# A convolution and top-1 mixture of experts on one core: closer expert steps in a fixed VectorE order, two small tiles after chunk 5, and one softmax maximum more

## The chip, the core and the metric

The kernel runs on one core of a Trainium2 chip. The metric is the device time of one execution in microseconds (us), the median of several runs. The engines are TensorE (PE, whose weight loads the profile lists apart as PEld), VectorE (DVE), ScalarE (ACT), GpSimd (POOL) and the DMA queues that SyncE (SP) and GpSimd feed.

## The reference

28672 tokens of 192 channels pass a causal convolution of seven taps whose weights are drawn per token and head (8 heads of 24 channels) and softmaxed over the taps. Its result goes through a mixture of eight experts, of which each token takes the one with the largest gate logit:

```
w = exp(weight_gen - max(weight_gen, -1)); w = w / (sum(w) + 1e-9)
x = einsum('bshk,bskhg->bshg', w, x_unf)          # conv, tokens x 192
expert_idx = argmax(x @ w_gate); gate_w = softmax(x @ w_gate)[expert_idx]
y[token] = gate_w * (max(x @ w1[e], 0) @ w2[e])   # e = expert_idx, 192 -> 1024 -> 192
```

## The kernel before, in words

**Chunks.** The tokens are worked in 28 chunks of 1024 (128 partitions times 8 columns). For chunk c, `soft0` takes the maximum over the taps on VectorE (L322) and subtracts it on GpSimd (L323), ScalarE takes the exponent (L326), VectorE sums and inverts (L331 to L336) and multiplies the weights (L344). The tap products are L355. In chunks 0 to 3 VectorE multiplies six of eight columns (128x1152), PE adds the products (L364) and GpSimd does the other two columns; from chunk 4 on VectorE does all columns (128x1536) and the additions too (L379). ScalarE squares the input for a scale (L414) and writes the high half of the result in 16 bits (`high`, L445 to L454; L449 in the chunks from 4 on), VectorE the low half (`low`, L462 and L464), PE transposes them (L474, copied by ScalarE in L476) and makes the logits (L486). `route1` (L493 to L508), `ranks` (L513, L515 on PE), `gate` (L522 to L529) and `places` (L536 to L545) find each token's place in its expert's queue in DRAM, and `send` scatters the tokens there with eight DMAs of GpSimd (L560). Last, `choose` picks by `select` (L574 to L606, which ends with `posn`) the rows at which the next tiles begin: a tile is T tokens of one expert.

**Tiles.** `make_plan` fixes ahead of time how many tiles of which T follow each chunk: while more than 8 x (T-1) tokens are pending, one of the experts must have T, and a tile is taken. Chunks 1 to 4 (`EARLY` is 5) give tiles of 256, the later ones of 384, the last chunk the rest with 128. Before, 13 tiles of 256 follow chunks 1 to 4, none chunk 5, three of 384 chunk 6, two chunk 7, three chunks 8 and 9, two chunk 10 and so on; in all 97 tiles. For each tile `fetch` loads the tokens transposed (xt<-queue, L744), the expert's weights (wt<-wq, 1.8 MB, L746) and the tokens' numbers (L749), on SP's queue. A tile of 256 then has four groups, one of 384 eight: PE does the first layer (40 matmuls a tile in L806), ScalarE the rectified high half (hh), and the low half (hl) comes from VectorE (L829), or, in every third tile and in tiles of chunks before `EARLY`, from PE and ScalarE (L815, a correction by a negated identity, negi, L819, and L821). L712 is the second layer, L716 ScalarE's scaling, and L560 scatters the output rows.

**The weights' stage.** Each expert's weights are split once into a high and a low half of 16 bits. `w_load` (L236 to L244) loads them, into three buffers (`PROB`), `w_norm` squares them on PE (L262) with a reduction on VectorE (L263), `w_high` has a matmul (L269), four small VectorE rows (L210 to L213 and L271) and two copies by ScalarE (L272, L273), `w_low` two long VectorE rows (L279, L281), and then SP writes the result to DRAM as wq. A tile's wt<-wq reads one expert's 128 rows of it, at an offset known only at run time, so it waits for the writes of all eight.

**What sets the order.** `vector_step` is a planner: it keeps two clocks in units of about a microsecond (`clock[0]` for VectorE, `clock[1]` for PE) and at each call emits the next piece that is due, in this order of preference: a low half of a tile (`pend`), an event of the weights' stage, a route, a split, the convolution. Expert e's three events are due at `W_AT + W_GAP*e`, `W_HIGH` and `W_LOW` later. While the weights' stage lasts, the planner is called in a plain loop, and VectorE's rows are then put in another order by an automatic scheduler, as on the other engines. After it, VectorE's program order is kept as written (`manual_schedule`).

In `sums`, chunk c+1's `soft0` comes at the second tap step while c+1 < `MX_FROM`+2, and from chunk `MX_FROM` on chunk c+2's comes at tap step `MX_AT`, 11. Chunk 3 has only eight tap steps, and with `MX_FROM` 3 chunk 5's `soft0` comes at neither place: its maximum is left out (the exponent is taken of the weights as they are).

Of the kernel before, what the change touches and what calls it, by code (L numbers as in the profile page):

```python
# [20 lines left out]
E = 8  # L21
# [13 lines left out]
EARLY = 5  # L35
# [11 lines left out]
SHRINK = 1.0 - 2.0 ** -11  # L47
FETCH = 16.0
W_AT = 10.0
W_GAP = 11.0  # L50
W_HIGH = 4.0
W_LOW = 8.0
T_MAIN = 384
# [2 lines left out]
MX_AT = 11  # L56
EXP_AT = 4
SC_AT = 7
MX_FROM = 3
FRONT = 10  # L60
SQ = 4
PROB = 3
# [10 lines left out]


def t_main(c, last):
    if c < 1:
        return []
    if c < EARLY:
        return [256]
    if c < last:  # L80
        return [T_MAIN]
    return [T_MAIN, 256, 128]


def make_plan(n_chunks, chunk):


    events, pending = [], 0

    def full(ev, T):  # L90
        nonlocal pending
        s = 0
        while pending > E * (T - 1):
            pending -= T
            s += 1
        if s:
            ev.append((T, s, None))

    for c in range(n_chunks):
        pending += chunk  # L100
        ev = []
        for T in t_main(c, n_chunks - 1):
            full(ev, T)
        events.append(ev)


    T = 128
    n = (pending + E * (T - 1)) // T
    ends = [min(T, pending // k if k <= E else (pending - T * (k - E)) // E) for k in range(1, n + 1)]
    events[-1].append((T, n, [-(-m // T_STEP) * T_STEP for m in ends]))  # L110
    return events
# [3 lines left out]
def conv_moe_kernel(ctx: ExitStack, tc: tile.TileContext, x, wgen, w_gate, w1, w2, out):  # L115
# [4 lines left out]
    NCH = NP // J  # L120
# [198 lines left out]
    def soft0(c):  # L319
        k = ch[c]  # L320
        mx = cw.tile([P, J * H], F32, name="mx")
        nc.vector.tensor_reduce(mx, k.w, axis=AX.X, op=ALU.max)  # L322
        nc.gpsimd.tensor_tensor(k.w, k.w, mx.unsqueeze(2).to_broadcast([P, J * H, KW]), op=ALU.subtract)  # L323

    def soft1(c):
        nc.scalar.activation(ch[c].w, ch[c].w, AF.Exp)  # L326
# [282 lines left out]
    todo = []  # L609
# [51 lines left out]
    def sums():  # L661
# [9 lines left out]
        for c in range(NCH):  # L671
# [4 lines left out]
            for cost in taps(c):  # L676
# [5 lines left out]
                if c + 1 < NCH:  # L682
                    if n == 2 and c + 1 < MX_FROM + 2:
                        soft0(c + 1)
                        yield 0.6, None
                    if n == EXP_AT:
                        soft1(c + 1)
                    if n == MX_AT and MX_FROM <= c < NCH - 2:

# [65 lines left out]
    def experts():  # L755
# [8 lines left out]
        n = 0  # L764
# [11 lines left out]
        def flush():  # L776
            while outs:
                idx, o = outs.pop(0)
                scatter(out, idx, o, "o", bound=N - 1)

        while True:
# [6 lines left out]
            T, xt, wt, meta = loaded.pop(n)  # L788
# [6 lines left out]
            for t in range(groups):  # L795
                if t:
                    yield None, 0.0
                f0 = t * fg
                flush()
                while len(pend) > 3:  # L800
                    low_part()
                ph = ps_h.tile([P, fg, T], F32, name="ph")
                for g in range(fg):
                    f = f0 + g
                    for k, (wc, xc) in enumerate(((0, 0), (0, 2), (O_L0, 0), (O_H1, 1), (O_L1, 1))):
                        nc.tensor.matmul(ph[:, g], wt[:, wc + f * P:wc + (f + 1) * P], xt[:, xc, 0:T],  # L806
                                         start=(k == 0 and g == 0), stop=(k == 4),
                                         skip_group_check=g > 0)
                hv, lv = hh[:, f0:f0 + fg], hl[:, f0:f0 + fg]
                while subs:  # L810
                    subs.pop(0)()
                if (n % 3 == 1 or todo[n][3] < EARLY) and todo[n][3] < NCH - 1:


                    nc.scalar.activation(hv, ph, AF.Relu, scale=SHRINK)  # L815

                    def rest(ph=ph, hv=hv, lv=lv, fg=fg):
                        for g in range(fg):
                            nc.tensor.matmul(ph[:, g], negi, hv[:, g], start=False, stop=True,  # L819
                                             skip_group_check=True)  # L820
                        nc.scalar.activation(lv, ph, AF.Relu)  # L821

                    subs.append(rest)
                    clock[1] += T * fg * (6 + 4.5) / 2400.0 + 15 * fg * MM
                else:
                    nc.scalar.activation(hv, ph, AF.Relu)  # L826

                    def lo(ph=ph, hv=hv, lv=lv):
                        nc.vector.scalar_tensor_tensor(lv, ph, 0.0, hv, op0=ALU.max, op1=ALU.subtract)  # L829
                        return (T * fg + 60) / 960.0  # L830

                    cost = T * fg * (5 + 4.5) / 2400.0 + 14 * fg * MM
                    clock[1] += cost
                    pend.append((clock[1] + LATE, n, lo))
                if t > 0 or groups == 1:
                    while pend and pend[0][1] < n:
                        low_part()
                    m = -(-left // (groups - t))
                    second(m)
                    left -= m  # L840
                if t == groups - 1:
                    p = min(P, T)
                    nc.scalar.activation(fac[0:p, 0:T // p], meta[0:p, 0:T // p, 0], AF.Copy,
                                         scale=wt[0:p, O_INV:O_INV + 2].bitcast(F32))
                if t >= 1 and len(done_) < len(todo):
                    m = len(done_)
                    if m <= n + 2 or (todo[m][3] == NCH - 1 and m <= n + AHEAD + 2):
                        loaded[m] = fetch(m)
                        done_.append(m)
# [10 lines left out]


    plan = make_plan(NCH, J * P)
    clock = [0.0, 0.0]

    def low_part():
        at, _, lo = pend.pop(0)
        clock[0] = max(clock[0], at) + lo()

    def weights(pro):

        ev = []
        for e in range(E):
            at = W_AT + W_GAP * e
            ev += [(at, e, 0), (at + W_HIGH, e, 1), (at + W_LOW, e, 2)]
# [15 lines left out]
    wstream = [None, 0.0]  # L890
# [56 lines left out]
    with tc.tile_pool(name="pro", bufs=PROB) as pro, tc.tile_pool(name="pro1", bufs=1) as pro1:  # L947
        stats = [pro1.tile([P, 2], F32, name=f"st{e}") for e in range(E)]
        stage = [pro1.tile([P, W_STAGE], F16, name=f"ws{i}") for i in range(PROB)]
        for t in stage:  # L950
            nc.gpsimd.memset(t[:, W_INV:W_INV + 16], 0.0)
        load(0)
        for e in range(len(stage)):
            w_load(e, pro)
            if e == 0:
                load(1)
        wstream[0] = weights(pro)
        clock[0] = 5.0
        while wstream[0] is not None:
            vector_step()  # L960
    with tc.manual_schedule(engines={mybir.EngineType.DVE}):
        ffw = ctx.enter_context(tc.tile_pool(name="ffw", bufs=3, reuse_waits="tile"))
        ffx = ctx.enter_context(tc.tile_pool(name="ffx", bufs=2, reuse_waits="tile"))
# [4 lines left out]
        n, _ = next(parts)  # L968
        while n is not None or parts is not None:
# [11 lines left out]
            n, _ = parts.send(True)  # L981
# [23 lines left out]
```

## Time and profile before

| | before |
|---|---|
| median of 3 runs | 1224.63 us (1223.89 to 1232.61) |
| the profiled execution | 1224.1 us |
| its span in the profile | 1222.4 us |
| mean granted TensorE clock | 0.976 of full speed |
| DMA | 320.94 MB, mean 263 GB/s |

The profile comes from one execution, and its times count from the start of the span. Busy time is summed over an engine's instructions; a mean of one instruction is in ns, and "x" counts them. A note in square brackets is the idle time of the engine just before the row and what ended it. PEclk is the granted clock as a share of 2.4 GHz.

### The profile page before, as it was taken

Reading aid. Unit: us, or ns where it says so; the run is one execution under the profiler, and the core shown is the slowest. Engines: PE = TensorE matmul, PEld = TensorE weight load, DVE = VectorE, ACT = ScalarE, POOL = GpSimd, SP = SyncE. Lnnn points to the kernel's source line nnn. Section 1 sums busy time; section 2 is a strip of 40 time slices with the busy share of each in tenths; the row PEclk is TensorE's granted clock in tenths of the full one; section 3 lists DMA queues with packets and bytes.
Section 4 is the critical chain, followed back from the end, with each engine's and each line's share of the span. In section 5 each row is a group of like instructions: output and inputs, shape, how many; then the busy total and the mean of one; then the engine's idle time right before and its main releaser. Section 6 shows DMA issues by size and latency. Waiting matters only on the chain.

```text
span 1222.4 us, 30194 instructions
## 1 busy us (share of the span) xinstructions
PE 1143.8 (94%) x11666; PEld 933.4 (76%) x11666; DVE 1025.9 (84%) x1840; ACT 697.5 (57%) x1467; POOL 660.1 (54%) x575
## 2 busy tenths in 40 slices
PE   5689189999999999999999999999999999999997
PEld 3456179988878787878778787878788776789997
DVE  7989969998999999999999999999999965232331
ACT  3556257767566656666666566656655663443442
POOL 6875526576464666455565546564547766222222
PEclk9989589999999999999999999999999999999999
DMA  9978879889878787777887877788766667999995
GB/s 275 358 275 286 295 224 296 285 284 283 293 225 230 233 268 258 228 238 230 249 262 232 266 215 246 236 263 258 239 198 201 210 198 234 353 321 359 323 336 236
DMA packets 185134, 320.94 MB, mean 263 GB/s; under 512 B 132752, under 2 KB 156434, under 8 KB 169118
## 3 DMA queue, kind: packets, MB, share of 16 engines
q1 hardware_dynamic: 162862, 273.68, 71.4%
q0 software_dynamic: 22128, 45.33, 11.1%
q8 instruction: 91, 1.49, 0.5%
q14 instruction: 53, 0.43, 0.1%
HBM read 236.17 MB, written 60.76 MB: 243 GB/s over the span
## 4 chain that ended last, share of the span: by engine, by line
PE 66%; issue 14%; DMA 8%; POOL 5%; DVE 4%; ACT 1%; SPq 1%; POOLq 0%; DVEq 0%; ACTq 0%
PE ph L806 30%; PE y L712 27%; POOL out_dram L560 4%; DMA wt<-wq 4%; PE ph L474 3%; PE ph L819 2%; PE ph L364 2%; DMA f<-in_moe_w_dram 1%; DVE tv L355 1%; POOL queue L560 1%; PE pm L486 1%; DVE ws L281 1%; DMA queue<-padrow,padi 1%; DMA x_sb<-in_x_dram 1%; DMA queue<-pl,pos 1%
## 5 line engine op out<-in xcount | busy, mean ns | idle before, releaser
L806 PE MATMUL ph<-xt,wt 128*128 128x384 f16 (+6 forms) x3880 | 581.3, 293 | 22.2 <-DMA wt<-wq 18.6
L712 PE MATMUL y<-wt,hh 128*128 128x192 f16 (+2 forms) x3696 | 505.8, 246 | 0.0
L560 POOL DMA_INDIRECT out_dram<-o,meta x231 | 285.7, 1237 | 379.4 <-ACT o L716 339.4
L712 PE MATMUL y<-wt,hl 128*128 128x192 f16 (+2 forms) x1848 | 450.7, 246 | 0.0
L806 PEld LDWEIGHTS <-wt 128*128 128x128 f16 x3880 | 331.0, 98 | 140.8 <-DMA wt<-wq 21.3
L712 PEld LDWEIGHTS <-hh 128*128 128x128 f16 (+2 forms) x3696 | 336.6, 98 | 33.4 <-issue 0.5
L560 POOL DMA_INDIRECT queue<-pl,pos x224 | 276.5, 1234 | 120.2 <-issue 63.8
L829 DVE SCALAR_TENSOR_TENSOR hl<-ph,hh 128x384 f16<-128x384 f32 (+2 forms) x372 | 203.3, 559 | 136.3 <-ACT hh L826 130.7
L355 DVE TENSOR_TENSOR tv<-x_sb,wp 128x1536 f32<-128x1536 f32 (+1 forms) x172 | 287.2, 1674 | 8.0 <-PE ph L364 7.7
L826 ACT ACTIVATE hh<-ph 128x384 f16<-128x384 f32 (+2 forms) x372 | 185.6, 501 | 186.2 <-PE ph L806 178.5
L379 DVE TENSOR_TENSOR acc<-acc,tv 128x1536 f32<-128x1536 f32 x144 | 250.0, 1736 | 0.0
L712 PEld LDWEIGHTS <-hl 128*128 128x128 f16 (+2 forms) x1848 | 181.5, 98 | 15.7 <-ACT hl L821 0.4
L815 ACT ACTIVATE hh<-ph 128x384 f16<-128x384 f32 (+1 forms) x204 | 105.2, 518 | 78.3 <-PE ph L806 69.4
L716 ACT ACTIVATE o<-y,fac 128x192 f32<-128x192 f32 (+2 forms) x231 | 92.5, 419 | 82.0 <-PE y L712 78.7
L821 ACT ACTIVATE hl<-ph 128x384 f16<-128x384 f32 (+1 forms) x204 | 104.3, 520 | 37.8 <-PE ph L819 37.1
L476 ACT ACTIVATE xg<-ph 128x1024 f16<-128x1024 f16 x84 | 84.5, 1028 | 31.9 <-PE ph L474 30.0
L364 PE MATMUL ph<-tv,identf 128*128 128x384 f32 x168 | 68.1, 544 | 14.6 <-DVE tv L355 10.7
L819 PE MATMUL ph<-hh,negi 128*128 128x384 f16 (+1 forms) x256 | 68.9, 305 | 4.7 <-ACT hh L815 4.6
L364 PEld LDWEIGHTS ph<-tv,identf 128*128 128x128 f32 x168 | 32.8, 210 | 34.9 <-DVE tv L355 13.3
L414 ACT ACTIVATE junk<-x_sb 128x768 bf16<-128x768 f32 (+2 forms) x56 | 48.0, 857 | 14.4 <-DVE ssq L423 6.8
L474 PE MATMUL ph<-idh,pl 128*128 128x128 f16 x672 | 53.4, 220 | 1.2 <-ACT xg L476 0.5
L449 ACT ACTIVATE pl<-acc 128x768 f16<-128x768 f32 (+1 forms) x52 | 40.0, 811 | 21.0 <-DVE acc L379 16.3
(121 smaller groups left out, 805.1 us busy)
## 6 DMA issues: line engine op xcount, KB each, us to landing
wt<-wq SPq DMA_DIRECT2D x97, 1796.0 KB
x_sb<-in_x_dram SPq DMA_DIRECT2D x27, 1344.0 KB
w_sb<-in_weight_gen_dram SPq DMA_DIRECT2D x28, 224.0 KB
wq<-ws SPq DMA_DIRECT2D x8, 772.0 KB
f<-in_moe_w_dram SPq DMA_DIRECT2D x8, 768.0 KB
f<-in_moe_w_dram SPq DMA_DIRECT2D x8, 512.0 KB
wq<-ws SPq DMA_DIRECT2D x8, 512.0 KB
wq<-ws SPq DMA_DIRECT2D x32, 128.0 KB
```

The costliest lines, as they stand in the source:

```text
L355: eng.tensor_tensor(out, xs, ws, op=ALU.mult)
L364: nc.tensor.matmul(ap[:, 0:m], identf, tf[:, 2 * i * D:2 * i * D + m], start=(n == 0), stop=(n == KW - 1))
L379: eng.tensor_tensor(ac, ac, t, op=ALU.add)
L560: st = nc.gpsimd.indirect_dma_start(out=dst, out_offset=bass.IndirectOffsetOnAxis(ap=idx, axis=0), in_=src, in_offset=None, **kw)
L712: nc.tensor.matmul(y, hx[:, f, sl], w2v[:, f, t, :], start=(f == 0 and k == 0), stop=(f == NF - 1 and k == 2))
L716: nc.scalar.activation(o[0:m, :], y, AF.Copy, scale=fac[0:m, s:s + 1])
L806: nc.tensor.matmul(ph[:, g], wt[:, wc + f * P:wc + (f + 1) * P], xt[:, xc, 0:T], start=(k == 0 and g == 0), stop=(k == 4), skip_group_chec ...
L815: nc.scalar.activation(hv, ph, AF.Relu, scale=SHRINK)
L819: nc.tensor.matmul(ph[:, g], negi, hv[:, g], start=False, stop=True, skip_group_check=True)
L821: nc.scalar.activation(lv, ph, AF.Relu)
L826: nc.scalar.activation(hv, ph, AF.Relu)
L829: nc.vector.scalar_tensor_tensor(lv, ph, 0.0, hv, op0=ALU.max, op1=ALU.subtract)
```

## The change

Seven edits in three parts. The weights' stage: experts stand 9 units apart, not 11, and the planner's loop stands in `manual_schedule`, so that VectorE's program order is kept there as the planner emits it. The plan: `t_main` now gives pairs of a T and a largest number of tiles, and chunk 5 gives up to two tiles of 256; the other chunks' limit of 99 is never reached. After it the plan has 15 tiles of 256 up to chunk 5, one of 384 after chunk 6, three after chunks 7 and 8, two after chunk 9, three after chunks 10 and 11 and so on, 98 tiles in all; the first tile of chunks 7, 10, 13, 16, 19, 22 and 25 has 256 tokens fewer ahead of it than before, that of the others 128 more. Tiles of chunk 5 count as early, so their low halves come from PE and ScalarE. Third, `MX_FROM` is 4, so chunk 5's softmax maximum is taken.

```diff
-W_GAP = 11.0
+W_GAP = 9.0
-MX_FROM = 3
+MX_FROM = 4
 def t_main(c, last):
...
     if c < EARLY:
-        return [256]
+        return [(256, 99)]
+    if c == EARLY:
+        return [(256, 2)]
     if c < last:
-        return [T_MAIN]
-    return [T_MAIN, 256, 128]
+        return [(T_MAIN, 99)]
+    return [(T_MAIN, 99), (256, 99), (128, 99)]
...
-    def full(ev, T):
+    def full(ev, T, most):
...
-        while pending > E * (T - 1):
+        while s < most and pending > E * (T - 1):
...
-                if (n % 3 == 1 or todo[n][3] < EARLY) and todo[n][3] < NCH - 1:
+                if (n % 3 == 1 or todo[n][3] <= EARLY) and todo[n][3] < NCH - 1:
...
-        while wstream[0] is not None:
-            vector_step()
+        with tc.manual_schedule(engines={mybir.EngineType.DVE}):
+            while wstream[0] is not None:
+                vector_step()
```

The lines of the changed kernel stand 3 further on from `soft0` to the tiles' first groups (L355 is L358 there, L279 is L282), and 4 at the end.

The first place is VectorE around the last expert's split, the two rows into ws1. Before (x_sb_706 is chunk 4's input):

```order
L355 TENSOR_TENSOR tv_1414<-x_sb_706,wp_1366 128x1536
L279 SCALAR_TENSOR_TENSOR ws1_178<-f1_942,nsc_1283,ws1_178 128x1536
L505 TENSOR_REDUCE pmx_1204<-pri_1202 128x8
L524 TENSOR_SCALAR se_1224<-se_1224 128x8
L281 SCALAR_TENSOR_TENSOR ws1_178<-f2_943,nsc_1283,ws1_178 128x8x192
L508 TENSOR_TENSOR oh0_108<-pri_1202,pmx_1204 128x64
```

And of the change (x_sb_407 is chunk 3's input, w_sb_795 chunk 4's tap weights):

```order
L325 TENSOR_REDUCE mx_1181<-w_sb_795 128x64
L358 TENSOR_TENSOR tv_1187<-x_sb_407,wp_1119 128x1152
L282 SCALAR_TENSOR_TENSOR ws1_178<-f1_853,nsc_1125,ws1_178 128x1536
L284 SCALAR_TENSOR_TENSOR ws1_178<-f2_854,nsc_1125,ws1_178 128x8x192
L358 TENSOR_TENSOR tv_1220<-x_sb_407,wp_1119 128x1152
L496 TENSOR_REDUCE lg_1250<-pm_1225 128x64
L499 TENSOR_REDUCE lm_1253<-lg_1250 128x8
```

Before, the last split stands among the products of chunk 4 and inside chunk 2's route; now it stands among those of chunk 3 and ahead of the whole of chunk 2's route, which then follows in one piece.

The second place is ScalarE around chunk 4's high half (into pl1). Before (hh_1534 and hl_1535 belong to tile 0, hh_1631 and hl_1632 to tile 1):

```order
L821 ACTIVATE hl_1535<-ph_1609 128x2x256
L815 ACTIVATE hh_1631<-ph_1633 128x2x256
L815 ACTIVATE hh_1631<-ph_1646 128x2x256
L449 ACTIVATE pl1_132<-acc_1365 128x4x192 x2
L815 ACTIVATE hh_1631<-ph_1707 128x2x256
```

And of the change (hh_1787 and hl_1788 belong to tile 2, fac_1786 too):

```order
L818 ACTIVATE hh_1787<-ph_1807 128x2x256
L417 ACTIVATE junk_1784,ssqs_161<-x_sb_1364 128x768
L824 ACTIVATE hl_1788<-ph_1792 128x2x256
L824 ACTIVATE hl_1788<-ph_1807 128x2x256
L846 ACTIVATE fac_1786<-meta_1578,wt_1576 128x2
L329 ACTIVATE w_sb_1365<-w_sb_1365 128x448
L452 ACTIVATE pl1_132<-acc_1368 128x4x192 x2
```

The high half stood behind the first two groups of tile 1 and stands now behind the first two of tile 2.

## Rows read from the trace of the kernel before

**Rows 1.** The page, part 1: busy time, share of the span, instructions.

```profile
PE 1143.8 (94%) x11666; PEld 933.4 (76%) x11666; DVE 1025.9 (84%) x1840; ACT 697.5 (57%) x1467; POOL 660.1 (54%) x575
```

**Rows 2.** Windows: stretch, length, busy time of PE, PEld, DVE, ACT, POOL, PEclk, DMA, GB/s.

```profile
134.00:165.00 31.00, 11.79 (x100) 9.12 (x101) 24.75 (x53) 7.32 (x15) 21.42 (x17) 0.61 0.87 289
0.00:300.00 300.00, 232.66 (x2151) 186.74 (x2152) 270.18 (x465) 169.28 (x309) 185.88 (x180) 0.91 0.88 288
300.00:1000.00 700.00, 699.87 (x6956) 558.22 (x6954) 679.43 (x1210) 435.37 (x950) 404.73 (x325) 1.00 0.78 238
```

**Rows 3.** PE in order of time, the first tile: start, us, row, idle before.

```profile
149.86 5.95 PE L806 MATMUL ph<-xt,wt 128*128 128x256 f16 x32 [11.90 <-DMA wt<-wq]
```

**Rows 4.** DVE in order of time, five places of the first 300 us.

```profile
21.64 1.35 DVE L355 TENSOR_TENSOR tv<-x_sb,wp 128x1152 f32<-128x1152 f32 x1 [2.62 <-PE ph L364]
...
131.32 1.80 DVE L281 SCALAR_TENSOR_TENSOR ws<-f,nsc,ws 128x1536 f16<-128x1536 f32 x1
...
141.56 0.15 DVE L606 SCALAR_TENSOR_TENSOR posn<-cnt,posn 1x8 f32<-1x8 f32 x1
...
169.83 0.69 DVE L462 TENSOR_TENSOR pl<-acc,pl 128x512 f16<-128x512 f32 x1 [10.40 <-ACT pl L449]
...
297.64 0.15 DVE L606 SCALAR_TENSOR_TENSOR posn<-cnt,posn 1x8 f32<-1x8 f32 x1
```

**Rows 5.** Windows of L806 alone: stretch, length, PE, PEld, PEclk, DMA, GB/s.

```profile
149.00:164.00 15.00, 6.98 (x40) 5.03 (x41) 0.73 0.89 299
186.60:290.90 104.30, 51.44 (x400) 38.14 (x400) 1.00 0.90 290
290.90:329.05 38.15, 22.21 (x120) 11.40 (x121) 1.00 0.87 282
770.20:905.00 134.80, 75.25 (x400) 37.64 (x401) 1.00 0.78 242
```

**Rows 6.** The chain that ended last, 170 to 335: a weights' load.

```profile
282.69 8.21 DMA wt<-wq
```

**Rows 7.** Groups by line and shape: busy, mean ns of one, idle before.

```profile
L355 DVE TENSOR_TENSOR tv<-x_sb,wp 128x1152 f32<-128x1152 f32 x28 | 37.3, 1337 | 7.8 <-PE ph L364 7.7
L355 DVE TENSOR_TENSOR tv<-x_sb,wp 128x1536 f32<-128x1536 f32 x144 | 249.9, 1739 | 0.2
L322 DVE TENSOR_REDUCE mx<-w_sb 128x64 f32<-128x448 f32 x27 | 16.4, 608 | 0.3 <-DMA w_sb<-in_weight_gen_dram 0.3
L323 POOL TENSOR_TENSOR w_sb<-w_sb,mx 128x448 f32<-128x448 f32 x27 | 27.2, 1006 | 40.2 <-DVE mx L322 38.3 <-DVE pl L527 1.9
L819 PE MATMUL ph<-hh,negi 128*128 128x256 f16 x104 | 20.0, 275 | 4.7 <-ACT hh L815 4.6
```

**Rows 8.** Waits of DVE, 60 to 134: total us, times, longest.

```profile
DVE tv L355 <- PE ph L364: 5.1, 4, 2.0
DVE pl L462 <- ACT pl L449: 0.9, 1, 0.9
DVE ws L279 <- ACT ws L272: 0.5, 1, 0.5
DVE se L522 <- ACT eg L499: 0.4, 1, 0.4
```

**Rows 9.** POOL in order of time: last scatters of chunks 7, 19 and 23.

```profile
301.39 0.96 POOL L560 DMA_INDIRECT queue<-pl,pos  x1 [0.30 <-issue]
...
746.26 2.99 POOL L560 DMA_INDIRECT queue<-pl,pos  x1 [0.30 <-issue]
...
891.25 0.96 POOL L560 DMA_INDIRECT queue<-pl,pos  x1 [0.30 <-issue]
```

More of the change, by code (lines that the diff above doesn't have):

```diff
@@ L101, in make_plan @@
         ev = []
-        for T in t_main(c, n_chunks - 1):
-            full(ev, T)
+        for T, most in t_main(c, n_chunks - 1):
+            full(ev, T, most)
         events.append(ev)
```

## The prediction

> **What bounds the kernel now.** I read the page's first part, then the windows, then inside the first 330 us TensorE's and VectorE's rows in order of time. The page: PE is busy 94% of the span, DVE 84% [rows 1]. The windows say where the missing PE time lies: from 300 to 1000 us PE is busy 699.87 of 700 us, so there only less PE work could save time; in the first 300 us it is busy 232.66, so 67.3 us are idle, while DVE is busy 270.18 [rows 2]. What counts here is therefore how early the expert tiles start and whether they find their tokens. The first tile's matmul starts at 149.86, after 11.90 us of idle PE that ended with the weights' load from DRAM (wt<-wq) [rows 3]. That load needs all eight experts' split weights, and the last split's VectorE instruction, L281 of expert 7, ends at 131.32+1.80=133.1 [rows 4]; 149.86-133.1=16.8 us for its writes and the load follow. From 186.6 on, ten tiles of 256 tokens take 104.3 us, 10.4 each; three of 384 take 38.15, 12.7 each [rows 5]. The matmuls of the first kind fill half of their time: those tiles are paced by their weights' load, 8.21 us in the chain [rows 6].
>
> **The weights' stage in a fixed order.** The diff puts VectorE in program order there and draws experts together (9 units apart, not 11). Counting what stands ahead of the last split in the two orders: five tap products of 1152 columns, five operations of 1536 (a first product, three products, one addition), one softmax product and 21 small ones have moved behind it; nothing has moved ahead. That is 5x1.337=6.7, 5x1.739=8.7, .6 for the softmax product (priced as the maximum over the same 448 columns, 608 ns) [rows 7], and 21 small ones at .21, an estimate between posn's .15 and the 512-column .69 [rows 4] and near the former as most hold 8 to 64 columns: 4.5. Sum 20.5 us.
>
> Against it stand waits. The old order put each row where its operands were ready; from 60 to 134 us VectorE waited 5.1+.9+.5+.4=6.9 [rows 8]. In a fixed order a row whose operand is late holds all rows behind it. I see three such places: expert 1's high step, which needs PE behind chunk 2's squares on ScalarE; chunk 0's logits behind the squares of expert 3's weights; chunk 2's logits. No row of before shows those waits. Bounds: nothing waits, -6.9; or all eight norms and four logits wait as long as the longest wait for PE that is shown, 2.62 [rows 4]: 12x2.62-6.9=+24.5. I take three at 2.62 (7.9) and .9, twice the .4 row and a little, in each of three routes now run in one piece (2.7): 10.6-6.9=+3.7. The last split then ends at 133.1-20.5+3.7=116.3 (105.7 to 137.1), and the first tile starts 16.8 later, at 133 instead of 150.
>
> The Trainium skill (Perfetto Trace Analysis, "Tensor Engine Instruction (MATMUL, LD_WEIGHTS)") says that ScalarE, VectorE and GpSimd are strictly first-in first-out. The 10.40 us below agrees; read to its end the rule speaks against the change, since every late norm would hold a whole queue: that is the third rival.
>
> **Tokens for the tiles that come earlier.** Tile 1 needs chunk 2's scatters. Chunk 2's choice stands behind one tap product, the logits' wait and 23 small rows: 116.3+1.3+2.6+.9+23x.21=126. Chunk 7's choice ends at 297.79 and its last scatter at 301.39+.96=302.35 [rows 4, 9], 4.6 later, so 130.6, and with the 8.21 load 139. The first tile's 40 matmuls took 6.98 [rows 5], so PE is there at 140 (before: 164.0). Up to chunk 3's choice both orders hold the same rows but for one large product fewer (1.7) and one maximum more (.6): that maximum (chunk 5's, now taken) costs .6 of VectorE, and a subtraction of 1.0 on GpSimd [rows 7], which is busy 54% [rows 1]; if that cover failed it would be 1.0. Chunk 3's choice moves from 141.71 to 141.7-1.1+3.7+2.6 (its own logits)=146.9, bounds 133.7 to 165.1. Then chunk 4's taps: VectorE reached their split 17.7 us after that choice (159.43) and waited 10.40 for ScalarE's L449 [rows 4], which stood behind tile 1's second group in ScalarE's order. Now it stands behind tile 2's second, about 140+10.4+5=155, and VectorE comes at 146.9+17.7+1.7=166.3: the wait goes, and chunk 4's split is 3.5 us earlier (16.7 earlier to 14.7 later). What is late next is VectorE itself. The two tiles after chunk 5 add one selection, eight small rows, 1.7. So at chunk 7's choice VectorE is 1.8 ahead (15.0 ahead to 16.4 behind).
>
> **The two small tiles and the sum.** PE has 15 tiles of 256 instead of 13, then one of 384 instead of three, before chunk 7's first. From 140: 14 tiles at 10.4, one at 12.7, so PE arrives at 298.5. Chunk 7's rows: scatters end at 302.35-1.8=300.6. From a scatter's end to the tile's start takes between the bare load, 8.21 [rows 6], and chunk 23's 905.0-(891.25+.96)=12.8, where PE didn't wait [rows 5, 9]. I take 11, in the middle: start at 311.6. PE waits 13 us there. Before, that tile began at 329.05 after 13x256+3x384=4480 tokens; now after 4224, and 256 tokens are 12.7x256/384=8.5. So 320.5 against 311.6: 8.9 gained. What it costs: after the 11.90 us of idle PE the granted clock was .61 in 134 to 165 [rows 2, 3], in part the lower of the two levels (1.2 and 2.4 GHz); .73 over the first tile's 15 us [rows 5] means about 8 us at the lower level, and I take some 4 us of busy PE that lose half, 2 (0 to 4). More PE work: three tiles of 256 for two of 384 are 120x.129-80x.188=.4 [rows 5], and 16 further corrections by PE (L819) at .19, 3.1, for eight of 1.5 times the columns, 2.3, that go [rows 7]: .8. One more 1.8 MB load lies under PE at a DMA share of .78 [rows 2]. Gain 8.9-2-1.2=5.7.
>
> The profiled execution took 1224.1 us, its span 1222.4; that is .5 under the runs' median of 1224.63, which the range covers. Forecast: 1224.1-5.7=**1218.4 us**.
>
> The Trainium skill (TensorE: Matmul & The Clock Gate, "HAM oscillation — how this bites in real kernels") says that gaps between bursts of matmuls send the engine back to the half-rate clock, each burst paying anew. The .61 above agrees. By it the gap before chunk 7 costs the 2 that is in the sum, and would be paid again at each further gap: the second rival.
>
> **Rivals.** *The waits are small.* Five places at .5, as the smaller rows 8: 2.5-6.9=-4.4. Chunk 4's split is then at 141.7-1.1-4.4+19.4=155.6, 14.2 ahead, 12.5 at chunk 7: ready at 300.9, PE waits 2 and keeps its clock. 320.5-300.9-1.2=18.4: **1206**. For: the shown waits for ScalarE are .4 to .9. Against: PE and ScalarE run queues of their own in this stage.
>
> *Given back at chunk 19.* There the first tile also comes 256 tokens earlier in the plan. Its scatters end at 746.26+2.99=749.25, ready at +12.8=762.05; it began at 770.2 [rows 5, 9]: slack 8.2. If VectorE stays only 1.8 ahead, PE must wait 8.9-1.8+8.5-8.2=7.4. Gain 8.9-7.4-1.2-4 (two stretches at the lower level)=-3.7: **1227.8**. For: DVE is busy 679.43 of 700 [rows 2]. Against: the 20.6 us left are just what it can regain.
>
> *The slower side: norms that stall the queue.* Each of the twelve places waits 2.62. VectorE is 16.4 behind at chunk 7: ready at 302.35+16.4+11=329.8, against 320.5: -9.3-4-1.2=-14.5: **1238.6**. It decides from 5.7 us more waiting than in my sum on. For: fewer units between experts leave ScalarE less time per expert. Against: ScalarE is busy 57% [rows 1], and none of the waits in rows 8 exceeds 2.0.
>
> **Chances.** Forecast .52 (own range 1211 to 1223), small waits .22, given back .16, stalled queue .10. The range, 1206 to 1230, reaches the first two rivals and leaves most of the third and half of the small waits out. One per cent, 12.2 us, is about what a measurement of this kernel can tell from no change. Faster by more (under 1211.9): the .22 and .03 of the forecast's edge, .25. Slower by more (over 1236.3): .07 of the third rival and .01 of the second, .08. Between: .67.
>
> **What would show it.** Right: the last split ends near 116, the first tile starts near 133, no wait of 10 us before chunk 4's split, chunk 7's choice near 296, and before chunk 7's first tile a PE gap near 13 us with a lower clock behind it. The small waits' rival shows the last split before 109 and no such gap; the second a gap near 770 or later; the third many VectorE waits over 2 us for PE in the first 130 us. I am wrong if the first tile moves by under 8 us, or if PE's work after 330 us changes by more than 3.

## The result: 1.5% slower, and the profile after

| | before | after |
|---|---|---|
| median | 1225.14 us (4 runs) | 1243.56 us (4 runs, 1241.46 to 1249.85) |
| ratio | | 1.0145, 95% interval 1.0105 to 1.0184 |
| span of the profiled execution | 1222.4 us | 1239.8 us |

The forecast was 1218.4, with a range up to 1230. The time lies beyond the slower rival's 1238.6, to which I had given .10. Measured again later, against 13 runs of before, the same kernel took 1247.25, ratio 1.0175 (1.0132 to 1.0219).

One thing is needed to read the numbers below: in the first, second and fifth series of experiments the kernel before itself took 1349 to 1353 us (called the long condition below), so a ratio from those series can't be set beside one from the others.

The page's first part after, which answers to [rows 1]:

```profile
PE 1153.6 (93%) x11714; PEld 943.1 (76%) x11714; DVE 1030.1 (83%) x1846; ACT 696.8 (56%) x1464; POOL 678.8 (55%) x576
```

Windows of after (columns as in [rows 2]): up to the last expert's split, up to chunk 3's choice, the first 142 us, and the steady part with the four stretches in which PE is not full:

```profile
0.00:126.70 126.70, 84.88 (x495) 54.90 (x495) 101.64 (x181) 56.02 (x84) 82.37 (x100) 0.85 0.93 300
0.00:165.00 165.00, 113.59 (x735) 76.29 (x736) 128.63 (x249) 74.14 (x120) 98.95 (x117) 0.86 0.91 291
0.00:142.00 142.00, 90.96 (x538) 58.85 (x539) 110.69 (x207) 58.49 (x88) 92.91 (x111) 0.84 0.93 297
300.00:1000.00 700.00, 691.73 (x6877) 552.39 (x6875) 687.73 (x1209) 430.21 (x938) 420.15 (x320) 1.00 0.78 240
300.00:350.00 50.00, 46.96 (x506) 39.95 (x504) 46.94 (x82) 32.73 (x67) 30.21 (x23) 1.00 0.89 300
350.00:400.00 50.00, 48.97 (x471) 38.17 (x470) 49.19 (x89) 30.84 (x70) 30.94 (x24) 1.00 0.72 218
850.00:900.00 50.00, 46.74 (x479) 37.55 (x478) 49.18 (x94) 29.55 (x64) 28.64 (x24) 1.00 0.80 258
900.00:950.00 50.00, 49.20 (x480) 38.34 (x478) 50.00 (x86) 29.72 (x64) 32.69 (x24) 1.00 0.68 188
```

The same three early windows of the kernel before, for the comparison:

```profile
0.00:133.10 133.10, 90.27 (x576) 57.84 (x577) 117.39 (x210) 65.35 (x104) 86.47 (x106) 0.91 0.89 296
0.00:141.70 141.70, 92.02 (x618) 59.36 (x618) 125.15 (x249) 65.70 (x105) 91.48 (x111) 0.89 0.89 293
0.00:142.00 142.00, 92.02 (x618) 59.36 (x618) 125.45 (x249) 65.70 (x105) 91.50 (x112) 0.89 0.89 292
```

The reader should look at VectorE. Chunk 3's choice is its 248th instruction in both kernels (the windows count one more, which has just begun): done at 141.7 before and at 165.0 now. Busy up to it: 125.15 and 128.63; idle: 141.7-125.15=16.6 and 165.0-128.63=36.4. So 19.8 of the 23.3 us are idle time, and 3.5 are longer busy time. In the same 142 us VectorE did 125.45-110.69=14.8 us less work. What it waited for stands in its waits up to 165:

```profile
DVE tv L358 <- PE ph L367: 13.8, 10, 2.9
DVE lg L496 <- PE pm L489: 8.1, 2, 4.4
DVE ssq L426 <- ACT junk L417: 2.9, 1, 2.9
DVE mx L325 <- DMA w_sb<-in_weight_gen_dram: 2.6, 1, 2.6
DVE rk L539 <- PE pm L518: 2.0, 1, 2.0
```

Before, up to 141.7, the tap products' waits for PE's sums were 7.7 and there was none for the logits:

```profile
DVE tv L355 <- PE ph L364: 7.7, 5, 2.6
DVE ssq L423 <- ACT junk L414: 2.4, 1, 2.4
```

In order of time on VectorE, the places spoken of (the norm that I had feared, chunk 0's and chunk 2's logits, the last split, a product that waits for PE, the choice of chunk 3, chunk 4's split, the choice of chunk 7):

```profile
39.76 0.16 DVE L213 TENSOR_SCALAR nbits<-y 128x2 int32<-128x2 int32 x1 [0.45 <-PE y L272]
...
55.50 0.29 DVE L496 TENSOR_REDUCE lg<-pm 128x64 f32<-128x128 f32 x1 [3.71 <-PE pm L489]
...
124.14 2.55 DVE L284 SCALAR_TENSOR_TENSOR ws<-f,nsc,ws 128x1536 f16<-128x1536 f32 x1
...
132.37 0.29 DVE L496 TENSOR_REDUCE lg<-pm 128x64 f32<-128x128 f32 x1 [4.42 <-PE pm L489]
...
143.76 1.35 DVE L358 TENSOR_TENSOR tv<-x_sb,wp 128x1152 f32<-128x1152 f32 x1 [2.95 <-PE ph L367]
...
164.87 0.15 DVE L609 SCALAR_TENSOR_TENSOR posn<-cnt,posn 1x8 f32<-1x8 f32 x1
...
185.31 0.69 DVE L465 TENSOR_TENSOR pl<-acc,pl 128x512 f16<-128x512 f32 x1 [0.90 <-ACT pl L452]
...
314.67 0.15 DVE L609 SCALAR_TENSOR_TENSOR posn<-cnt,posn 1x8 f32<-1x8 f32 x1
```

And on PE, chunk 3's tap sums, the first tile, chunk 4's transposes and the first tile of chunk 7:

```profile
139.61 9.93 PE L367 MATMUL ph<-tv,identf 128*128 128x384 f32 x24 [5.01 <-DVE tv L358]
...
151.80 1.25 PE L809 MATMUL ph<-xt,wt 128*128 128x256 f16 x10
...
185.33 0.29 PE L477 MATMUL ph<-idh,pl 128*128 128x128 f16 x1 [9.69 <-ACT pl L452]
...
333.01 0.99 PE L809 MATMUL ph<-xt,wt 128*128 128x384 f16 x5 [2.45 <-DMA wt<-wq]
```

The last split does end earlier, at 124.14+2.55=126.7 (before: 133.1 by [rows 4]), but the first tile starts at 151.80, 2 us later than before: in PE's order it stands behind chunk 3's tap sums, which waited 5.01 for VectorE and then took 9.93 us. The tile's weights were there by 138.9, when ScalarE's row that reads them (L846) ran. Chunk 7's first tile starts at 333.0 after 4224 tokens; before at 329.05 after 4480. That is 3.9+8.5=12.4 us lost. Windows from the first tile to chunk 7's first tile, now and before:

```profile
151.80:333.00 181.20, 162.72 (x1825) 149.13 (x1822) 173.40 (x285) 120.62 (x237) 102.85 (x77) 0.96 0.82 264
149.86:329.05 179.19, 169.70 (x1805) 149.93 (x1806) 163.37 (x257) 119.11 (x241) 100.64 (x78) 0.97 0.86 277
```

PE is idle there for 18.5 us now and 9.5 before, and more than half of the 18.5 is one wait, the 9.69 us at 185.33: in PE's order chunk 4's transposes come next, they need ScalarE's high half (L452), and VectorE ended the last product of chunk 4 only at 184.4. So what VectorE's lateness costs the tiles shows already at chunk 4, long before chunk 7.

In the steady part PE lacks 700-691.73=8.3 (before: .1), nearly all of it in the four stretches shown, where the longest gaps (2.45 at 333.0, 1.94 at 883.9) end with a tile's weights' load. The gap of 2.45 lies ahead of chunk 7's first tile and is in the 12.4 already, as part of the 33.00-30.57=2.4 that PE lacks from 300 to 333; from there to 1000 it lacks 5.8. Together that is 12.4+5.8=18.2, for 17.4 by which the span grew.

### The profile page after: what moved, and what is told of

The parts are those of the page before. It is cut to its first block, busy times and chain, and to the rows that moved or that the text cites. A ratio compares the mean times of both kernels' runs of the same rounds, so it can differ in the third digit from the quotient of the medians.

```text
span 1239.8 us, 30313 instructions
## 1 busy us (share of the span) xinstructions
PE 1153.6 (93%) x11714; PEld 943.1 (76%) x11714; DVE 1030.1 (83%) x1846; ACT 696.8 (56%) x1464; POOL 678.8 (55%) x576
## 4 chain that ended last, share of the span: by engine, by line
PE 70%; DMA 10%; issue 8%; DVE 6%; POOL 3%; ACT 1%; SPq 1%; POOLq 0%; DVEq 0%; ACTq 0%
PE ph L809 33%; PE y L715 29%; DMA wt<-wq 4%; DMA wq<-ws 3%; PE ph L477 3%; POOL out_dram L563 3%; PE ph L822 3%; DMA f<-in_moe_w_dram 1%; PE ph L367 1%; DVE tv L358 1%; PE pm L489 1%; DVE ws L282 1%; DMA x_sb<-in_x_dram 1%; DVE ws L284 1%; DVE hl L832 1%
## 5 line engine op out<-in xcount | busy, mean ns | idle before, releaser
L809 PE MATMUL ph<-xt,wt 128*128 128x384 f16 (+7 forms) x3920 | 577.2, 290 | 15.3 <-DMA wt<-wq 12.7
L563 POOL DMA_INDIRECT out_dram<-o,meta x231 | 289.8, 1255 | 382.5 <-ACT o L719 328.6
L563 POOL DMA_INDIRECT queue<-pl,pos x224 | 286.7, 1280 | 102.9 <-issue 59.7
L358 DVE TENSOR_TENSOR tv<-x_sb,wp 128x1536 f32<-128x1536 f32 (+1 forms) x172 | 287.7, 1676 | 14.2 <-PE ph L367 13.8
L715 PEld LDWEIGHTS <-hl 128*128 128x128 f16 (+2 forms) x1848 | 181.4, 98 | 15.8 <-ACT hl L824 0.7
L367 PE MATMUL ph<-tv,identf 128*128 128x384 f32 x168 | 69.7, 570 | 13.6 <-DVE tv L358 13.6
L367 PEld LDWEIGHTS ph<-tv,identf 128*128 128x128 f32 x168 | 35.8, 223 | 37.3 <-DVE tv L358 14.9
L417 ACT ACTIVATE junk<-x_sb 128x768 bf16<-128x768 f32 (+2 forms) x56 | 48.1, 859 | 15.2 <-DVE ssq L426 10.4
L477 PEld LDWEIGHTS <-pl 128*128 128x128 f16 x672 | 43.6, 100 | 16.7 <-ACT pl L452 9.9
```

The costliest lines, as they stand in the source:

```text
L358: eng.tensor_tensor(out, xs, ws, op=ALU.mult)
L367: nc.tensor.matmul(ap[:, 0:m], identf, tf[:, 2 * i * D:2 * i * D + m], start=(n == 0), stop=(n == KW - 1))
L477: nc.tensor.transpose(pt[:, m, :], p16[:, j, n * P:(n + 1) * P], idh)
L563: st = nc.gpsimd.indirect_dma_start(out=dst, out_offset=bass.IndirectOffsetOnAxis(ap=idx, axis=0), in_=src, in_offset=None, **kw)
L715: nc.tensor.matmul(y, hx[:, f, sl], w2v[:, f, t, :], start=(f == 0 and k == 0), stop=(f == NF - 1 and k == 2))
```

## The experiments

Theory A: the fixed VectorE order in the weights' stage is the loss. Theory B: the plan with two small tiles is. The first four kernels undo or do one part each.

**auto**, the changed kernel with the order given back to the scheduler:

```diff
-        with tc.manual_schedule(engines={mybir.EngineType.DVE}):
-            while wstream[0] is not None:
-                vector_step()
+        while wstream[0] is not None:
+            vector_step()
```

> The changed kernel with the weights' stage's VectorE order given back to the scheduler; closer experts, two small tiles and the extra maximum stay. Theory A (the fixed order makes VectorE wait for PE: chunk 3's choice came at 165.0 instead of 141.7, and the 14 to 17 us that VectorE lags at chunks 4 to 7 are the loss): chunk 3's choice back before 148, time 1216 to 1228. Theory B (the plan costs it: more tiles, more corrections on PE, one selection more): chunk 3's choice before 148 too, but the time stays at 1236 or above.

**manual_only**, the kernel before with only that `with` added:

```diff
-        while wstream[0] is not None:
-            vector_step()
+        with tc.manual_schedule(engines={mybir.EngineType.DVE}):
+            while wstream[0] is not None:
+                vector_step()
```

> The kernel before with the fixed VectorE order alone (experts 11 apart, no small tiles, chunk 5's maximum still left out). Theory A: chunk 3's choice at 158 or later, time 1236 to 1246. Theory B: within 5 us of before, 1220 to 1230.

**nosmall**, the changed kernel without the small tiles:

```diff
-    if c == EARLY:
-        return [(256, 2)]
...
-                if (n % 3 == 1 or todo[n][3] <= EARLY) and todo[n][3] < NCH - 1:
+                if (n % 3 == 1 or todo[n][3] < EARLY) and todo[n][3] < NCH - 1:
```

> The changed kernel without chunk 5's two small tiles (fixed order, experts 9 apart, extra maximum). Theory A: the lag of VectorE stays, so 1238 to 1250; above the changed kernel if the small tiles covered part of the lag. Theory B: 1223 to 1230.

**small_only**, the changed kernel with all but the small tiles undone (auto's edit, and these):

```diff
-W_GAP = 9.0
+W_GAP = 11.0
-MX_FROM = 4
+MX_FROM = 3
```

As in the kernel before, chunk 5's softmax maximum is then left out, and in manual_only too.

> The kernel before with chunk 5's two small tiles alone. Theory A: within 5 us of before, 1220 to 1230. Theory B: 1234 to 1245.

Measured against before in the same series (1353.36): auto 0.9903 (0.9847 to 0.996), manual_only 1.008 (1.0041 to 1.0119), nosmall 1.003 (1.0 to 1.0061), small_only 1.017 (1.0106 to 1.0234). No absolute time expected here applies, since before itself took 1353. The ratios speak for both theories at once: the order costs, the small tiles too, though auto, which has the small tiles, lies below before. So I repeated them.

> The same kernel as auto, for a chip on which the kernel before takes about 1225 us, as in the profiles the prediction was made from. Theory A (the fixed order is the loss): chunk 3's choice before 148, 1212 to 1228. Theory B (the plan is the loss): 1236 or above.

> The same kernel as manual_only. Theory A: chunk 3's choice at 158 or later, 1234 to 1246. Theory B: 1220 to 1230.

> The same kernel as nosmall. Theory A: 1236 to 1250. Theory B: 1223 to 1230.

> The same kernel as small_only. Theory A: within 5 us of before, 1220 to 1230. Theory B: 1234 to 1245, with chunk 6's choice 10 us or more later than before's 267.3.

Again before took 1349.11: auto 0.9928 (0.9885 to 0.9971), manual_only 1.0101 (1.006 to 1.0141), nosmall 1.0081 (1.0034 to 1.0129), small_only 1.017 (1.0126 to 1.0214). The sequence repeats, but so does the long condition, and theory B's ratio for small_only could be a property of it.

The third series had the changed kernel itself, and **gapmx**, the kernel before with experts 9 apart and chunk 5's maximum:

```diff
-W_GAP = 11.0
+W_GAP = 9.0
-MX_FROM = 3
+MX_FROM = 4
```

> The changed kernel itself, unedited, on the chip that this call gets. If that chip is like the two of the earlier calls (the kernel before at about 1350 us, engines stalled for 3 to 8 us at a time with no releaser named): the fixed order's own cost there was .8 to 1.0% (manual_only) and giving it back was worth auto's .7 to 1.0% below before, so theory A expects a ratio of 1.000 to 1.012; theory B, by small_only's 1.017, expects 1.015 to 1.035. On a chip like the first: 1.0145 again.

> The kernel before with experts 9 apart and chunk 5's maximum taken, VectorE's order left to the scheduler, no small tiles. Theory A: these two parts cost nothing, ratio 0.985 to 1.003. Theory B (the small tiles are what costs): 0.975 to 0.995, as auto without its small tiles.

Before took 1225.18. The changed kernel: 1.0175 (1.0132 to 1.0219), slower as on the first occasion. gapmx: 0.9994 (0.9974 to 1.0013). Without the fixed order these two parts cost and bring nothing. Its window up to chunk 3's choice, and chunk 7's choice:

```profile
0.00:152.54 152.54, 102.40 (x675) 67.52 (x676) 126.74 (x249) 69.33 (x112) 98.98 (x117) 0.90 0.93 312
```

```profile
299.04 0.15 DVE L606 SCALAR_TENSOR_TENSOR posn<-cnt,posn 1x8 f32<-1x8 f32 x1
```

Chunk 3's choice comes 10.8 us later than before, with VectorE idle for 152.54-126.74=25.8 us (9.2 more), and yet chunk 7's choice is only 1.4 late (299.19 against 297.79) and the time is the same. Between the two lay the 10.40 us wait before chunk 4's split [rows 4], which is gone in gapmx: some 9 us of lateness at chunk 3's choice only fill it. In the changed kernel 23.3 became 17.0, and in manual_only (below) 20.2 became 11.6. So idle time up to chunk 3's choice is not yet a loss; what is left of it behind chunk 4 can be.

The fourth series, before at 1222.9, tells A from B:

> The changed kernel without the fixed order in the weights' stage, for a chip where the kernel before takes about 1225. Theory A (the fixed order is the whole loss): VectorE idle under 20 us up to chunk 3's choice, ratio 0.990 to 1.003. Theory B (the small tiles cost): 1.010 or above.

> The kernel before with the fixed order alone. Theory A: VectorE idle for 33 us or more up to chunk 3's choice, which comes 15 us or more later than before's 141.7; ratio 1.010 to 1.025. Theory B: ratio under 1.005.

> The kernel before with chunk 5's two small tiles alone. Theory A: 0.995 to 1.006. Theory B: 1.010 or above. If PE then waits before chunk 7's first tile, since that tile comes 256 tokens earlier and VectorE no sooner, the price lies between 2 and 8 us.

Measured: auto 1.002 (0.9993 to 1.0046), manual_only 1.0101 (1.007 to 1.0131), small_only 1.0 (0.9981 to 1.002). All three ratios are as theory A expects, none as B. The 1.017 of small_only belongs to the long condition. The windows of manual_only's profile, up to chunk 3's choice and in the steady part:

```profile
0.00:161.86 161.86, 101.51 (x618) 66.85 (x618) 129.56 (x249) 66.55 (x105) 98.12 (x116) 0.82 0.86 269
300.00:1000.00 700.00, 699.56 (x6937) 557.45 (x6936) 686.34 (x1218) 436.53 (x952) 407.58 (x323) 1.00 0.79 240
```

Chunk 3's choice is reached at 161.86, and VectorE was idle for 161.86-129.56=32.3 us (expected: 33 or more; 15.7 more than before's 16.6). The last expert's split, the first tile and chunk 7's first tile, the last with the same tokens done as before:

```profile
143.11 1.79 DVE L281 SCALAR_TENSOR_TENSOR ws<-f,nsc,ws 128x1536 f16<-128x1536 f32 x1
...
163.61 0.61 PE L806 MATMUL ph<-xt,wt 128*128 128x256 f16 x2 [5.37 <-DMA wt<-wq]
...
340.07 0.33 PE L806 MATMUL ph<-xt,wt 128*128 128x384 f16 x1
```

Chunk 7's first tile is 340.07-329.05=11.0 us late; in the steady part PE is full (699.56 of 700), and the profiled span is 1232.1-1222.4=9.7 us longer. The loss of the early stage goes through to the end nearly as it is. It enters by another way than in the changed kernel: with experts 11 apart the last split ends at 144.9, 11.8 us later than before, the first tile starts 13.8 late, and from there to chunk 7's first tile no more is lost (176.5 us, before 179.2). In the changed kernel the closer experts keep the first tile near its old place, and the loss comes with the tokens, from chunk 4 on.

auto's profile shows what the other parts do without the fixed order, up to chunk 3's choice, then to 300, then steady:

```profile
0.00:150.65 150.65, 102.49 (x676) 66.89 (x677) 129.56 (x249) 69.55 (x112) 98.87 (x117) 0.90 0.93 311
142.00:300.00 158.00, 148.80 (x1656) 137.25 (x1657) 151.13 (x249) 109.68 (x213) 92.11 (x69) 0.97 0.86 287
300.00:1000.00 700.00, 694.30 (x6889) 552.12 (x6886) 682.25 (x1228) 431.78 (x946) 423.51 (x325) 1.00 0.78 237
```

```profile
142.74 0.39 PE L809 MATMUL ph<-xt,wt 128*128 128x256 f16 x1 [3.96 <-DMA wt<-wq]
...
314.36 0.33 PE L809 MATMUL ph<-xt,wt 128*128 128x384 f16 x1
```

The choice comes at 150.65 and VectorE's idle time up to it is 21.1: both miss my numbers (before 148, under 20) by a little, and the ratio stands where theory A had it. The first tile starts 7.1 us earlier than before, and at chunk 7's first tile PE is 329.05-8.5-314.36=6.2 us ahead. But in the steady part it then lacks 5.7 us, while VectorE is busy 682.25: the gain is given back, and the ratio is 1.002. I read this as VectorE setting the pace of the chunks behind the start; no run tests that reading by itself.

**after_tv3**, the changed kernel with one more buffer for the tap products:

```diff
-TV = 2
+TV = 3
```

> The changed kernel with three buffers for the tap products instead of two, so that VectorE may run one product further ahead of PE's sums. If VectorE's waits for those sums (13.8 us up to chunk 3's choice, 8 of them over .5) are the main part of the loss: chunk 3's choice 5 to 10 us earlier than the changed kernel's 165 to 166, ratio at least .005 below the changed kernel's. If the logits' waits and the order itself are (8 to 10 us, of which no buffer helps any): chunk 3's choice within 3 us, same ratio.

Its waits up to chunk 3's choice at 161.1:

```profile
DVE lg L496 <- PE pm L489: 10.7, 3, 6.5
DVE tv L358 <- PE ph L367: 3.2, 3, 1.7
DVE st L266 <- PE y L265: 3.0, 2, 2.5
```

The waits for tap sums have gone down (13.8 to 3.2), but those for the logits are 2.6 longer and the norms, which had not waited, now wait 3.0. Chunk 3's choice is at 161.1, 3.9 to 5.4 us earlier than in the changed kernel's two profiles (165.0 and 166.5), at the edge between my two readings; the ratio is 1.0167 (1.0135 to 1.02), between the changed kernel's two. So the buffer moves the choices less than the waits it removes (10.6), and the time not measurably. The miss is in my expectation that a wait taken away is time gained: what follows in the fixed order waits instead. The Trainium skill (Perfetto Trace Analysis, "Tensor Engine Instruction (MATMUL, LD_WEIGHTS)") calls VectorE strictly first-in first-out, and these three rows fit that.

The last series tried that for the logits, and a better kernel, with before at 1353.12 once more.

**after_rest**, the changed kernel with the first routes due later, and **tv3_rest** with TV = 3 besides:

```diff
-        yield max(0.0, ch[c].sent + REST1 - clock[0])
+        yield max(0.0, ch[c].sent + (12.0 if c < 4 else REST1) - clock[0])
```

> The changed kernel with the routes of chunks 0 to 3 due 12 units after their splits instead of 6, so that in the fixed order other work stands ahead of the logits that VectorE waited 8.1 us for. If those waits are the loss: VectorE idle 6 to 9 us less up to chunk 3's choice, chunk 7's choice 5 us or more earlier, ratio 1.005 to 1.011. If what counts is the rows that now stand behind the experts' splits, or the waits for the tap sums: the idle time goes to other waits and the ratio stays at 1.013 to 1.020.

> Both edits, three buffers for the tap products and later routes. If VectorE's waits in the fixed order are the whole loss: VectorE's gaps over .3 up to chunk 3's choice at 14 to 18 us (before: 14.4), busy by 142 us above 121, chunk 7's choice by 305, ratio 0.998 to 1.006. Otherwise 1.010 or above.

The ratios are 0.9972 (0.9937 to 1.0006) and 0.9943 (0.9914 to 0.9972), in the long condition, in which nosmall has 1.003 to 1.008, so they seem to help there; the changed kernel itself wasn't run in it, and what they do where before takes 1225 stays open. The waits up to chunk 3's choice can be read with some care: manual_only reaches that choice at 162.2 to 162.9 in the long condition and at 161.9 outside it, but auto at 154.2 to 156.9 and at 150.65. after_rest, up to chunk 3's choice at 172.6:

```profile
DVE tv L358 <- PE ph L367: 13.8, 10, 2.8
DVE se L525 <- ACT eg L502: 9.5, 2, 8.8
```

The 8.1 for the logits have become 9.5 for ScalarE's exponent, one instruction of the same route (L525 waits 8.8 at once), and in tv3_rest 11.6. VectorE's idle time up to the choice is 38.0 and 34.9 us, where the changed kernel has 36.4: it went to other waits, as the second reading had it. Chunk 7's choice, at 320.4 and 313.9, can't be set beside the changed kernel's 314.8, since that choice comes at 322.0 to 323.7 in manual_only in the long condition and at 309.4 outside it. What does come earlier is the first tile, at 139.4 and 139.6 (nosmall in the same condition: 151.1 to 155.5); whether the ratios come from there was not tested.

> The changed kernel without the two small tiles, on a chip like the first. If the small tiles are harmless (small_only 1.0000) and only the fixed order costs: at the changed kernel's ratio, 1.013 to 1.020. If they cost because VectorE is late (chunk 7's first tile is wanted 256 tokens, 8.5 us, sooner, and PE waits for it): at manual_only's, 1.006 to 1.012.

nosmall came out at 1.0058 (1.002 to 1.0097), in the long condition once more and like its earlier runs there, and so doesn't tell what the small tiles add to the fixed order outside it.

**gapmx_tv3**, the try at a faster kernel (gapmx with TV = 3):

> A try at a faster kernel: the kernel before with experts 9 apart, chunk 5's maximum and three buffers for the tap products, order left to the scheduler. If VectorE's waits for tap sums (6.6 us in gapmx) delay the tiles: 0.992 to 0.998. If the steady part, in which VectorE is busy 681 of 700 us, gives the gain back: 0.997 to 1.003.

1.0012 (0.9978 to 1.0046): nothing gained, though only the long condition was seen. Outside it no kernel of this study beats the kernel before by more than its interval.

## Why the prediction was wrong

**The step that failed is the sum of the waits in the fixed order**: "I take three at 2.62 (7.9) and .9 ... in each of three routes: 10.6-6.9=+3.7", with 2.6 more for chunk 3's logits, 6.3 up to its choice. Measured are 36.4-16.6=19.8, inside the bounds (+24.5), but near their far end. The three places that I named cost 8.6 together, near the 7.9 that I gave them: chunk 0's logits waited 3.71, chunk 2's 4.42 and expert 1's high step .45. What failed is the other side of the sum. Its -6.9 takes all of before's waits as gone, and 5.1 of them are those of the tap products for PE's sums, the largest wait in [rows 8]. They didn't go, they grew, from 7.7 to 13.8 up to chunk 3's choice: I had counted the tap products only as moved work. The two longest of them, 5.7 us, stand behind sums that PE made at the lower clock (last section). With two buffers between them VectorE and PE wait for each other in turn (VectorE 13.8 us for PE's sums, PE 13.6 for the products); with three VectorE's part is 3.2.

A second term stood at nothing. Added up one by one, the 248 instructions last 145.9 us before and 144.7 after, 1.1 less, as forecast. But VectorE's busy time grew by 3.5 and the pauses of under .15 us between its rows by 2.4, because a row that needs the one just ahead starts behind its end (L499 at 132.70 lasts .22, L501 starts at 132.95), and one that doesn't starts before it (L505 at 56.34 lasts .23, L213 starts at 56.48). The scheduler had mixed the chains of small steps with other work; the fixed order runs them in one piece and loses 4.6 us of the overlap (manual_only 4.6 too, auto with the scheduler's order 1.5). So the 23.3 us are 17.4 of waits over .15 us, 7.0 of lost overlap and pauses, and 1.1 less work. I had 6.3 and 1.1 less.

**The last split** was to end at 116.3 and ended at 126.7. The moved work was 117.39-101.64=15.8 by the windows, not 20.5: 29 rows fewer stand ahead of it (x210 and x181), not 32, and the last two split rows took 2.30 and 2.55 instead of 1.8. The rest, 126.7-(133.1-15.8)=9.4, is further idle time, where I had 3.7.

**The first tile** "starts 16.8 later" than the last split: it started 25.1 later. Its weights' load no longer ended last; PE's own order did, with chunk 3's tap sums ahead of the tile. I had carried the 16.8 over without asking what stands ahead of the tile on PE once the taps are late.

**Chunk 7** was to find VectorE 1.8 ahead; it was 314.82-297.79=17.0 behind, and the tile started 333.01-314.82=18.2 after the choice (I had 4.6+11=15.6). The third rival had 16.4 behind and a start at 329.8: its arithmetic was nearly right, its cause was not. It blamed the norms, and they hardly waited. The PE gap of 13 us that I forecast ahead of this tile was 2.45, at the full clock (1.00 from 300 to 350); the long gap came at chunk 4, and behind it, from 178 to 191, the granted clock is 0.50, the lower level.

**The small steps** held: the 10.40 wait before chunk 4's split is gone (.90 left). The extra maximum and the closer experts are hidden (gapmx 0.9994), and so are the small tiles without the fixed order (small_only 1.0).

**But the gain that I expected from the small tiles doesn't exist.** In small_only chunk 7's first tile starts at 320.33, 256 tokens earlier: 329.05-8.5=320.5, the same. PE had no earlier start there, and two more tiles of 256 at 10.4 each [rows 5] took the place of 512 tokens that cost 17 in tiles of 384: my 8.9 hung on the start at 133, not on the tiles. And where an earlier start does come (auto), it is given back, as the second rival had it, but not at its place: from 750 to 800, around chunk 19, auto's PE is full (50.00 of 50), and it is short in 300 to 400 (by 1.6) and in 850 to 950 (by 4.0).

**What stays open**: the changed kernel lies .4 to .7% above the fixed order alone (1.0145 and 1.0175 against 1.0101). Of the 1239.8-1232.1=7.7 us between the profiled spans, 333.0-(340.07-8.5)=1.4 are there at chunk 7's first tile, and 5.4 come behind it (PE lacks 5.8 there, in manual_only .4), in stretches in which VectorE lags and the first tile of some chunks is wanted 256 tokens sooner. That points to the small tiles, but no run outside the long condition shows it, and there is a rival: closer experts and the extra maximum, harmless without the fixed order (gapmx), were not run with it there. nosmall, which has them and no small tiles, reaches chunk 3's choice at 164.3 to 168.8 in the long condition, manual_only at 162.2 to 162.9.

## What to carry to other kernels

Fixing an in-order engine's program order means pricing every place at which it meets another engine, the running exchange through two buffers first of all, and not only the places where something looks late. A chain of small steps run in one piece costs twice: each step may have to wait for another engine (logits 4.42, ranks 1.95), and its rows no longer overlap with others. Don't take the waits of the old order as gone before you have asked what removes them.

Idle time of a producing engine is a loss only as far as the next stage had no slack for it: some 9 us were covered here. What was lost at the start of a stage that is full on PE appeared in the total nearly one to one (11.0 and 9.7 in manual_only), while a lead of 6.2 us on PE alone was given back (auto). Before removing a wait, ask what stands behind it in the same order: here the edit that removed 10.6 us of waits brought the stage's end forward by 4 to 5 us, and the one that removed 8.1 did not bring it forward.

## What the runs showed that I had not expected

The kernel before took 1353.36 us in one series and 1222.9 in a later one on the same chip. In the long condition's profiles rows last as long as ever (a product of 1536 columns 1743 ns), but the engines stand idle more: in manual_only PE is busy 647 us from 300 to 1000, outside that condition 700. VectorE shows waits of up to 8.7 us there (auto, second series) and PE of up to 4.3 (small_only) for which the profile names no releaser; in the profile of the kernel before such waits of these two engines are 1.1 at most. The cause stays open. In that condition small_only reads 1.017, and 1.000 outside it: a ratio to a kernel measured beside it did not protect from that.

PE's clock is part of the exchange between VectorE and PE. Over the first 142 us the granted clock is 0.84 in the changed kernel and 0.89 before, with about the same busy time (90.96 and 92.02). Three windows of the changed kernel, the first and the last at the lower level and the second at the full one, then six tap sums of PE in the first and in the second, then the product that waited for the slow ones:

```profile
92.50:105.90 13.40, 7.62 (x35) 5.04 (x36) 10.16 (x28) 6.08 (x4) 9.02 (x8) 0.50 1.03 344
123.00:126.00 3.00, 3.00 (x28) 1.97 (x26) 3.00 (x2) 1.02 (x1) 2.92 (x2) 1.00 0.28 103
133.50:143.00 9.50, 3.87 (x15) 2.27 (x15) 6.76 (x23) 0.81 (x3) 5.01 (x5) 0.50 0.86 304
```

```profile
101.73 4.15 PE L367 MATMUL ph<-tv,identf 128*128 128x384 f32 x6
...
123.23 2.15 PE L367 MATMUL ph<-tv,identf 128*128 128x384 f32 x6
```

```profile
105.92 1.35 DVE L358 TENSOR_TENSOR tv<-x_sb,wp 128x1152 f32<-128x1152 f32 x1 [2.73 <-PE ph L367]
```

Six sums take 4.15 us in the one and 2.15 in the other, and VectorE's two longest waits for sums, 2.73 here and 2.95 at 143.76, end with the first and the last window. The Trainium skill (TensorE: Matmul & The Clock Gate, "HAM oscillation — how this bites in real kernels") says that each gap between bursts is paid again at half rate; these windows and the 0.50 behind the 9.69 us gap agree. Added up over the trace, PE is busy for 39 us at the lower level, before for 27, and half of the 12 more, 6 us, is an estimate of what that work takes longer. How much of the 17.4 us of the span this makes stays open, since no run changes the clock alone.
